# Half of the first x through transposing transfers instead of TensorE, wq right behind them on the SP queue, and a new instruction order

## The chip, the cores and the metric

One core of a Trainium2 chip. The metric is the device time of one execution in microseconds (us): 265.26 us, the median of three runs of the kernel before (265.08 to 267.14). TensorE (PE) multiplies matrices from SBUF into PSUM banks, VectorE (DVE), ScalarE (ACT) and GpSimd (POOL) do the element-wise work, and SyncE (SP) issues transfers. PE, ACT, DVE and POOL each execute their own instructions in order; they meet at semaphores only.

## The reference

Two branches over the same 2048 x 512 input x, mixed per token:

```python
q, k, v = x @ wq, x @ wk, x @ wv          # 32 heads of 16, four segments of 512 tokens
for s in range(4):                        # per segment and head
    a_dot = softmax(q_s k_s^T * 0.25 + causal mask) v_s
    a_mem = (phi(q_s) M) / (phi(q_s) z + 1e-6)      # phi(t) = t + 1 if t > 0 else exp(t)
    o_s = sigmoid(beta) * a_mem + (1 - sigmoid(beta)) * a_dot
    M, z = M + phi(k_s)^T v_s, z + sum(phi(k_s))
a = concat(o) @ wo
b = (gelu(x @ w_gate) * (x @ w_up)) @ w_down        # 512 -> 1792 -> 512
g = sigmoid(sum(x * gate_w))
out = g * a + (1 - g) * b
```

All inputs and the output are bfloat16, the sums in PSUM float32.

## The kernel before

The kernel is built as a list of named tasks. A task is one or several instructions of one engine together with what they read and write. The text `ORDER` at the end of the file gives the order of all tasks, written out by hand: an entry such as `Q0_0:0` is a task and the PSUM bank it opens (there are four banks, `psD0` to `psD3`), and `Qev0_0:a` is a task and the engine that does it (a for ACT, d for DVE). `Emitter` puts each task's instructions on its engine in this order and adds a semaphore wait for each dependency that is not already covered. No planner decides anything when the kernel is built, so the order in the text is the order in which each engine works.

Work is done by segment (s = 0 to 3, 512 tokens each). `project(s)` makes K, Q and V: the tasks `K`, `Q`, `V` with segment and tile are PE matmuls, and `Kev`, `Qev`, `Vev` take them out of PSUM. `kpada` and `kpadb` are DVE copies of K with half the rows masked out. `attend(s, t)` makes scores (`st`, PE, into the four-bank tile psX), their exponentials (`exp`, ACT), the causal mask on the diagonal blocks (`msk`, POOL) and the product with V (`pv`, PE). `vsh` are transfers that put V a second time at the other half of the partitions. `glu_gate(s)` and `glu_up(s)` make the second branch: `G` tasks are PE, seven of them go raw to SBUF (`Gev`) and then through one large ACT instruction (`gelu`, L681), the other seven are read from PSUM by ACT (`gd`, L686). `outputs(s)` multiplies with w_down (`out`) and wo (`wo`), adds, and stores in `dma` tasks. `memory_read`, `memory_write` are the a_mem part (`nd`, `mz`, and the transposing transfers `ktr` and `otr`).

The steps at the start that the change touches:

- The projections need x with its 512 features on the partitions, so x has to be transposed into `xT`. Segments 1 to 3 are loaded by transposing transfers (`ld_xt`, L342 to L346): four for a segment, each of 512 tokens by 128 features, `DMA_TRANSPOSE` on SP.
- Segment 0 is loaded plain into a spare tile and transposed by PE: `ld_x0_0` (128 tokens, SP), `ld_x0_1` (128 tokens, ACT's queue), `ld_x0_2` (256 tokens, SP, behind wk's second half). The tasks `xtr0_01`, `xtr0_00`, `xtr0_10`, `xtr0_11` (L771) are four PE transposes of 128 x 128 each. The first digit is the half of the tokens, the second the half of the features. `xev0_..` (L779 on ACT, L780 on DVE) copy the four results from PSUM to `xT`.
- K of segment 0 is made in pieces (L472): `a` and `b` are the first 256 tokens with features 256 to 511 and 0 to 255, `c` the last 256 tokens. Each piece a or b has two matmuls of 256 columns, each piece c has four; the four tiles make 32 matmuls.
- The weights for Q come in two transfers on SP, `ld_wq0` and `ld_wq1`. SP holds wq0 until wk1 has landed and wq1 until wk0 has landed. wv is held until `x0_2` has landed. These holds are there in `ld_w(..., wait)`:

```python
ld_w("wq0", SP, wq[:, halves[0], :], wsrc(A_wq)[:, halves[0], :], [("wq", 0)], 0.25, ["wk1"])
ld_w("wq1", SP, wq[:, halves[1], :], wsrc(A_wq)[:, halves[1], :], [("wq", 1)], 0.25, ["wk0"])
ld_w("wv", SP, wv[:, :, 0:512], wsrc(A_wv), [("wv",)], 0.5, ["x0_2"])
```

Of the kernel before, what the change touches and what calls it, by code (L numbers as in the profile page):

```python
# [28 lines left out]
R_XT = 3  # L29
# [217 lines left out]
def _build(es, nc, A_x, A_wq, A_wk, A_wv, A_wo, A_beta, B_w_gate, B_w_up, B_w_down, gate_w, out):  # L247
# [69 lines left out]
    def bk(s):  # L317
        return ("bank", s)
# [40 lines left out]
    ld_w("x0_2", SP, pt[stage[0]][:, halves[1], :], xin0[:, halves[1], :], [("xs", 0, 2), ("xs", 0, 3)], 0.25)  # L359
    ld_w("gw", SP, gw4, gate_w.rearrange("(kb p) -> kb p", p=P), [("gw4",), ("gwz",)], 0.01)  # L360
    ld_w("wq0", SP, wq[:, halves[0], :], wsrc(A_wq)[:, halves[0], :], [("wq", 0)], 0.25, ["wk1"])
    ld_w("wq1", SP, wq[:, halves[1], :], wsrc(A_wq)[:, halves[1], :], [("wq", 1)], 0.25, ["wk0"])
    ld_w("wv", SP, wv[:, :, 0:512], wsrc(A_wv), [("wv",)], 0.5, ["x0_2"])
# [100 lines left out]
    def xk(s, i):  # L464
        return [("xT", s % R_XT, i), *([("xT", 0, i, "h0")] if s == 0 else [])]

    def project(s):
        b, b3 = s % 2, s % R_XT
        k0 = [Slot() for _ in range(4)]
        for nm, kbs, h in (("a", (2, 3), 0), ("b", (0, 1), 0), ("c", (0, 1, 2, 3), 1)) if s == 0 else ():  # L470
            for t in range(4):
                one(f"K0_{t}{nm}", PE, len(kbs) * T_MM / 2, [I(lambda e, t=t, i=i, h=h: e.matmul(  # L472
                    BK[k0[t].i][:, 256 * h:256 * h + 256], wk[:, i, t * 128:(t + 1) * 128], xT[0][:, i, 256 * h:256 * h + 256],
                    start=(i == 2 - 2 * h), stop=(i == 1 + 2 * h)), [("xT", 0, i, "h0"), ("wk", i),
                    *([("xT", 0, i)] if h else [])], [bk(k0[t])]) for i in kbs], opens=(nm == "a"))
# [292 lines left out]
    for h in range(2):  # L768
        for p in (1, 0):
            j = 2 * h + p  # L770
            one(f"xtr0_{h}{p}", PE, 4 * T_TR, [I(lambda e, q=q, kb=kb, j=j: e.transpose(  # L771
                XB[:, 1024 * j + (kb % 2) * 256 + (q % 2) * 128:1024 * j + (kb % 2) * 256 + (q % 2) * 128 + 128],
                pt[stage[0]][:, q, kb * 128:(kb + 1) * 128], ident[:, :]),
                [("xs", 0, 2 * h), ("xs", 0, 2 * h + 1), ("pt", stage[0]), ("ident",)], [("X", j)]) for kb in (2 * p, 2 * p + 1) for q in (2 * h, 2 * h + 1)])
            dst = xT[0][:, 2 * p:2 * p + 2, 256 * h:256 * h + 256]
            xin = XB[:, 1024 * j:1024 * j + 512].rearrange("p (k c) -> p k c", c=256)
            wr = [("xT", 0, kb, "h0") if h == 0 else ("xT", 0, kb) for kb in (2 * p, 2 * p + 1)]
            task(f"xev0_{h}{p}", [
                (ACT, 0.477, [I(lambda e, dst=dst, xin=xin: e.activation(dst, xin, ACTF.Copy), [("X", j)], wr)]),  # L779
                (DVE, 0.335, [I(lambda e, dst=dst, xin=xin: e.tensor_copy(dst, xin), [("X", j)], wr)])], L_DVE)  # L780
# [67 lines left out]
ld_x0_0 warm0 warm1:0 ld_x0_1 ident xtr0_01 ld_wk0 masks vones0 causal1 causal0 gwz ld_wk1 ld_x0_2 ld_wq0 xev0_01:d  # L848
ld_gw consts xtr0_00 K0_1a:1 K0_2a:2 K0_3a:3 K0_0a:0 ld_wq1 ld_wv ld_beta xtr0_10 xtr0_11 xev0_00:a K0_2b K0_3b K0_1b
K0_0b xev0_11:a xev0_10:d K0_0c Kev0_0:d kpadb0_0 kpada0_0 K0_3c Kev0_3:a K0_1c K0_2c Kev0_2:d Kev0_1:d kpada0_1  # L850
Q0_0:0 Q0_3:3 Qev0_0:a st0_0A exp0_0A ld_x1_1 ld_x1_0 ld_x1_2 ld_x1_3 gwtr:2 gwev Qev0_3:d phka0_0 Q0_1:1 V0_3b:0
V0_0b:2 V0_2a:3 Vev0_3b:d st0_0B Vev0_0b:d ld_wg0 V0_1a:0 V0_3a:2 phkb0_0 Vev0_2a:d Qev0_1:d Vev0_1a:d Vev0_3a:d
V0_2b:3 Q0_2:1 V0_0a:0 exp0_0B st0_0C exp0_0C V0_1b:2 Vev0_2b:d betab Qev0_2:d Vev0_1b:a bexp Q1_1:3 Q1_2:1 kpadb0_1
Vev0_0a:d causal msk0_0A phkc0_0 vsh0_00 vsh0_01 vsh0_20 Qev1_2:d st0_0D V1_2b:0 G0_1:2 G0_3:1 exp0_0D st0_0E
Vev1_2b:d kpada0_3 exp0_0E V1_3a:0 Vev1_3a:a kpada0_2 Gev0_1:d Gev0_3:d Qev1_1:d G0_5:2 G0_0:1 st0_1A G1_3:3 V1_1b:0
msk0_0B Gev0_5:d vsh0_21 Gev0_0:d Gev1_3:d msk0_0D gqa msk0_0C kpadb0_2 Vev1_1b:d msk0_0E pv0_0:21 exp0_1A st0_1B
gfull tp0_d00 kpadb0_3 V1_0a:3 G0_4:0 msk0_1A G1_0:2 Vev1_0a:d phka0_2 tp0_d01 Gev0_4:d exp0_1B st0_1C exp0_1C msk0_1B
msk0_1C phkb0_2 Q1_0:3 G0_2:1 V1_3b:0 gqb pvp0_00 Qev1_0:d Gev1_0:d Vev1_3b:d Gev0_2:d phkc0_2 ld_wu1 ld_wg1 ld_wu0
ktr0_1 ld_x2_0 st0_1D exp0_1D G1_2:3 K1_0:2 K1_3:0 Gev1_2:d Kev1_3:d st0_2A G0_6:1 V1_2a:3 Vev1_2a:d Gev0_6:d Kev1_0:a
gz0 msk0_1D pv0_1:20 exp0_2A st0_2B exp0_2B ktr0_2 tp0_d10 pvp0_01 tp0_d11 pvp0_10 K1_1:3 Q1_3:1 Qev1_3:d Kev1_1:d  # L860
kpadb1_3 gelu0 G0_7:2 G1_1:0 Gev1_1:d gd0_7 st0_2C G1_4:1 G0_13:3 ktr0_0 Gev1_4:d phka1_0 ld_x2_2 ld_x2_3 G0_9:0
G0_10:1 G0_12:2 gd0_9 gd0_10 gd0_13 gd0_12 G0_8:0 ld_x2_1 vsh1_21 phqa1_0 pvp0_11 vsh1_20 ld_wd1 G0_11:1 K1_2:3
kpadb1_1 ota0_0 Kev1_2:d gd0_8 gd0_11 U0_10:2 V1_0b:0 h0_10 exp0_2C U0_7:1 Q2_1:3 V1_1a:2 ktr0_3 phka1_2 kpada1_3
Vev1_0b:d h0_7 kpada1_2 Qev2_1:d Vev1_1a:a st0_2D exp0_2D U0_11:0 U0_2:1 h0_11 h0_2 phqa1_2 mz0:2 phkb1_0 mza0 phkc1_0
st0_2E U0_4:3 K2_0:0 U0_13:1 h0_4 h0_13 kpada1_0 kpadb1_0 Kev2_0:d exp0_2E st0_3A exp0_3A msk0_2A msk0_2B msk0_2C
msk0_2D msk0_2E U0_9:2 pv0_2:31 st0_3B phkb1_2 exp0_3B h0_9 tp0_d21 G1_5:0 U0_5:2 U0_8:1 Gev1_5:a gr0 phkc1_2 tp0_d20
st0_3C h0_8 K2_3:3 Kev2_3:d U0_3:0 h0_3 pvp0_21 kpada1_1 U0_6:1 h0_5 h0_6 exp0_3C phqb1_2 st0_3D Q2_0:3 Q2_3:0 U0_1:2
exp0_3D Qev2_3:a Qev2_0:d h0_1 pvp0_20 kpadb2_3 st1_0A V2_2b:1 U0_0:3 exp1_0A phqb1_0 h0_0 msk0_3A msk0_3B msk0_3C gz1
goa0 gob0 msk0_3D pv0_3:02 st1_0B exp1_0B tp0_d31 tp0_d30 K2_2:3 U0_12:2 Vev2_2b:d kpadb1_2 Kev2_2:d V2_0b:0 V2_2a:1
st1_0C Vev2_0b:a exp1_0C Vev2_2a:d kpada2_2 h0_12 kpada2_3 phqc1_2 G1_6:3 K2_1:0 Kev2_1:d V2_1b:1 msk1_0B st1_0D  # L870
exp1_0D ld_wd0 kpadb2_1 ktr1_1 vsh1_00 Gev1_6:a out0_1_0:2 out0_0_0:0 st1_0E out0_0_1 out0_1_1 V2_0a:3 exp1_0E
Vev2_1b:d mzq0 Vev2_0a:d out0_0_2 out0_1_2 msk1_0C msk1_0E msk1_0A msk1_0D goc0 G1_8:1 G1_7:3 kpada2_0 ota0_2 wev0_1:d
wev0_0:d gelu1 gd1_7 G1_10:2 ld_x3_2 ktr1_2 ktr1_0 phka2_0 G1_11:0 G1_13:3 vsh1_01 ld_wo ktr1_3 gd1_10 gd1_11 gd1_13
gd1_8 G1_12:2 gd1_12 G1_9:0 ota0_1 pvp0_31 phqc1_0 kpadb2_2 pvp0_30 st1_1A pv1_0:31 tp1_d01 Q2_2:2 Qev2_2:d tp1_d00
ota0_3 gd1_9 V2_3b:0 U1_2:1 U1_9:2 h1_2 Vev2_3b:d pvp1_01 h1_9 pvp1_00 exp1_1A st1_1B phkb2_0 exp1_1B out0_2_0:3
wo0_0:1 V2_1a:0 st1_1C msk1_1B exp1_1C nd1_1:2 out0_2_1 out0_2_2 oev0_0 st1_1D msk1_1C msk1_1A exp1_1D Vev2_1a:a
wev0_2:d ndp1_1 wo0_1:1 out0_3_0:3 V2_3a:2 st1_2A out0_3_1 nd1_3:0 oev0_1 Vev2_3a:a msk1_1D pv1_1:12 exp1_2A st1_2B
dma1 phkc2_0 kpadb2_0 ndp1_3 exp1_2B msk1_2B ld_x3_1 dma0 ld_x3_0 ld_x3_3 tp1_d10 phka2_2 tp1_d11 out0_3_2 pvp1_10
G2_2:0 G2_4:1 wev0_3:a Gev2_4:d Gev2_2:d st1_2C nd1_5:2 G2_0:3 ndp1_5 G2_3:1 G2_1:0 exp1_2C st1_2D exp1_2D msk1_2C
msk1_2A msk1_2D G2_5:2 Gev2_3:d Gev2_1:d Gev2_0:d Gev2_5:d nd1_0:1 G2_6:0 Gev2_6:d nd1_2:3 ndp1_0 ndp1_2 st1_2E  # L880
G2_11:2 wo0_2:0 oev0_2 wo0_3:1 oev0_3 G2_13:3 G2_7:0 G2_10:1 gelu2 gd2_13 gd2_11 G2_8:3 G2_9:2 gd2_10 gd2_7 gd2_8
gd2_9 G2_12:1 K3_0:0 U1_3:3 nd1_4:2 gd2_12 gr1 exp1_2E phqa2_0 pvp1_11 ota1_0 Kev3_0:d ndp1_4 U2_7:1 h1_3 h2_7 U2_11:0
U2_10:2 ota1_1 h2_11 h2_10 st1_3A U2_13:3 U1_4:1 phkb2_2 exp1_3A msk1_2E pv1_2:02 st1_3B phqb2_0 exp1_3B msk1_3B h2_13
h1_4 tp1_d21 tp1_d20 U1_1:3 h1_1 phkc2_2 U1_6:1 U2_9:2 st1_3C U1_8:0 h1_6 U2_3:3 U1_5:1 exp1_3C st1_3D exp1_3D h2_9
h1_8 pvp1_20 h2_3 mz1:2 msk1_3A h1_5 mza1 phqa2_2 msk1_3C U1_0:0 U1_13:3 h1_0 pvp1_21 h1_13 kpada2_1 st2_0A msk1_3D
K3_3:1 U1_7:2 Kev3_3:d pv1_3:03 tp1_d31 h1_7 phqb2_2 dma3 otr1_2 otr1_3 dma2 exp2_0A st2_0B exp2_0B U2_1:1 h2_1 ota1_2
# [26 lines left out]
oev2_2 dma11 dma10 out3_1_1 out3_1_2 msk3_3D otm3_2 otm3_1 wev3_1:a otm3_0 out3_3_0:1 pv3_3:32 out3_0_2 out3_3_1  # L913
wev3_0:a out3_2_0:0 out3_2_1 tp3_d30 tp3_d31 pvp3_31 pvp3_30 ota3_3 otm3_3 wo3_1:3 oev3_1 dma13 wo3_0:2 oev3_0
out3_3_2 out3_2_2 dma12 wo3_3b:3 wev3_3:d oev3_3b wo3_3a:2 wo3_3c:1 oev3_3a dma15b dma15a wev3_2:a oev3_3c dma15c
wo3_2:3 oev3_2 dma14
"""


# [26 lines left out]
```

## Time and profile before

| what | us |
|---|---|
| median of three runs | 265.26 (265.08 to 267.14) |
| the profiled execution, its whole time | 265.46 |
| its span, first to last instruction | 263.7 |
| PE busy in that span | 254.3 |
| DVE busy | 207.9 |
| ACT busy | 197.7 |
| POOL busy | 99.8 |
| DMA queue of SP: 15.68 MB, share of 16 engines | 23.6% |

The lower table is the start of the profiled execution, from the timeline and from the landings of the transfers (us from the start of the span).

| transfer | issue by its queue | landed |
|---|---|---|
| x0_0 (SP) | 0.79 | 3.57 |
| x0_1 (ACT's queue) | 0.78 | 3.74 |
| wk1 (SP) | 1.25 | 5.01 |
| wk0 (ACT's queue) | 1.21 | 5.30 |
| x0_2 (SP) | 1.71 | 5.97 |
| wq0 (SP) | 5.03 | 7.64 |
| wq1 (SP) | 5.89 | 9.88 |
| wv (SP) | 6.33 | 11.34 |
| four transposing transfers of segment 1 (SP) | 7.66, 8.92, 10.21, 11.52 | 11.92, 12.95, 13.64, 14.40 |
| first half of w_gate (SP) | 12.82 | 18.02 |
| four vsh (SP) | 19.70 to 21.75 | 21.89 to 23.82 |
| half of w_up (SP) | 22.40 | 27.57 |

The page gives busy time by engine, the span in 40 slices, the chain of work that ended last, and the costliest groups of instructions. A few PE records are missing in the trace (2775 matmuls are recorded, 2815 weight loads), so a matmul that is missing looks like a short gap of PE. The profiled time outside the span is 265.46 - 263.7 = 1.76 us.

### The profile page before, as it was taken

To read this page: it belongs to the slowest core of one execution; us is meant where nothing else is said; L and a number is where in the kernel's file an instruction comes from. 1 tells how busy PE (TensorE), PEld (TensorE's weight loads), DVE (VectorE), ACT (ScalarE), POOL (GpSimd) and SP (SyncE) were. 2 spreads that over 40 slices of the span, in tenths; PEclk is the share of its full clock that TensorE was granted. 3 is DMA by queue.
4 is the path that set the end of the run, shared out by engine and by line. 5 is a ranking of instruction groups with operands and counts; after the bars stand their busy time and mean duration, and the time that the engine had idled before them with its cause. 6 is when DMAs were issued, how large, how long until landed. Compare 5 with 4: busy or idle time off the path is not lost.

```text
span 263.7 us, 6622 instructions
## 1 busy us (share of the span) xinstructions
PE 254.3 (96%) x2775; PEld 120.4 (46%) x2815; DVE 207.9 (79%) x427; ACT 197.7 (75%) x159; POOL 99.8 (38%) x164
## 2 busy tenths in 40 slices
PE   7999999999999999999999999999999999999994
PEld 4554544444454444444444444444444444444442
DVE  1698979588985866885897999885799967799765
ACT  2487779979888897788967877666889877776611
POOL 5018362054424306440244456436525045264500
PEclk9999999999999999999999999999999999999999
DMA  5855675901015000403103000030143000003302
GB/s 165 221 155 153 197 208 81 290 0 33 1 42 132 0 2 1 102 0 72 31 2 74 9 2 11 22 75 0 22 97 47 0 22 4 2 0 63 80 2 80
DMA packets 31302, 16.50 MB, mean 63 GB/s; under 512 B 20776, under 2 KB 31272, under 8 KB 31272
## 3 DMA queue, kind: packets, MB, share of 16 engines
q1 hardware_dynamic: 30856, 15.68, 23.6%
q8 instruction: 22, 0.36, 0.6%
q10 hardware_dynamic: 416, 0.39, 0.4%
q14 instruction: 8, 0.07, 0.1%
HBM read 8.14 MB, written 2.10 MB: 39 GB/s over the span
## 4 chain that ended last, share of the span: by engine, by line
PE 91%; DVE 3%; DMA 3%; issue 2%; SPq 0%
PE psD L446 45%; PE psD L718 17%; PE psX L598 8%; PE psD L640 7%; PE psD L495 6%; PE psD L732 5%; DMA wq<-in_A_wq_dram 2%; DMA wk<-in_A_wk_dram 1%; PE psD L543 1%; DVE omem L557 1%; DVE ost L736 1%; DVE tT L526 0%; PE psD L573 0%; SPq L340 0%; DVE rcm L556 0%
## 5 line engine op out<-in xcount | busy, mean ns | idle before, releaser
L604 ACT ACTIVATE pt<-psX 128x2048 bf16<-128x2048 f32 x72 | 135.1, 1876 | 41.2 <-PE psX L598 41.0
L610 POOL TENSOR_TENSOR pt<-pt,ctri 128x256 bf16<-128x256 bf16 x128 | 92.2, 726 | 145.3 <-ACT pt L604 117.4
L446 PE MATMUL psD<-xT,wu 128*128 128x512 bf16 x213 | 52.4, 379 | 1.3 <-issue 0.9
L718 PE MATMUL psD<-wd,gb 128*128 128x512 bf16 x213 | 51.8, 379 | 1.2 <-issue 1.0
L446 PE MATMUL psD<-xT,wg 128*128 128x512 bf16 x214 | 51.3, 379 | 1.0 <-issue 0.5
L703 DVE TENSOR_TENSOR gb<-psD,gb 128x512 bf16<-128x512 f32 x56 | 37.4, 680 | 4.9 <-PE psD L446 4.7
L446 PEld LDWEIGHTS psD<-xT,wg 128*128 128x128 bf16 x224 | 20.7, 98 | 24.9 <-issue 1.9
L526 DVE STREAM_TRANSPOSE tT<-psD 128x512 f32<-128x512 f32 x32 | 22.3, 705 | 12.3 <-PE psD L640 12.2
L446 PEld LDWEIGHTS psD<-xT,wu 128*128 128x128 bf16 x224 | 20.6, 98 | 24.1 <-issue 1.7
L718 PEld LDWEIGHTS psD<-wd,gb 128*128 128x128 bf16 x224 | 20.3, 98 | 23.9 <-issue 2.8
L598 PE MATMUL psX<-qT,kD 32*128 32x192 bf16 (+7 forms) x512 | 28.5, 287 | 0.0
L640 PE MATMUL psD<-pt,vnat 64*17 64x128 bf16 (+7 forms) x512 | 18.7, 283 | 0.0
L651 DVE SCALAR_TENSOR_TENSOR ob<-tT,gq,rc 128x256 bf16<-128x256 f32 x32 | 17.8, 556 | 1.1
L495 PE MATMUL psD<-wv,xT 128*128 128x256 bf16 (+1 forms) x128 | 18.5, 273 | 0.0
L640 PE MATMUL psD<-pt,vsh 64*17 64x128 bf16 (+7 forms) x512 | 18.3, 283 | 0.0
L598 PEld LDWEIGHTS psX<-qT,kD 32*128 32x128 bf16 x512 | 8.2, 92 | 21.3 <-ACT pt L604 8.9
L440 DVE CAST gb<-psD 128x512 bf16<-128x512 f32 x24 | 16.0, 681 | 2.4 <-PE psD L446 2.4
L686 ACT ACTIVATE gb<-psD 128x512 bf16<-128x512 f32 x28 | 15.4, 594 | 3.1 <-PE psD L446 2.8
L736 DVE SCALAR_TENSOR_TENSOR ost<-psD,gtok,wds 128x512 bf16<-128x512 f32 (+2 forms) x18 | 12.2, 686 | 6.1 <-PE psD L732 5.3
L440 DVE CAST kT<-psD 128x512 bf16<-128x512 f32 x14 | 9.5, 687 | 8.5 <-PE psD L446 7.3
L446 PE MATMUL psD<-xT,wq 128*128 128x512 bf16 x61 | 15.5, 380 | 0.5 <-DMA wq<-in_A_wq_dram 0.2
L732 PE MATMUL psD<-wo,oT 128*128 128x512 bf16 (+2 forms) x71 | 15.8, 356 | 0.0
(84 smaller groups left out, 258.9 us busy)
## 6 DMA issues: line engine op xcount, KB each, us to landing
out_dram<-ost SPq DMA_DIRECT2D x15, 128.0 KB, 1.8
wg<-in_B_w_gate_dram SPq DMA_DIRECT2D x2, 896.0 KB, 6.3
wu<-in_B_w_up_dram SPq DMA_DIRECT2D x2, 896.0 KB, 5.1
wd<-in_B_w_down_dram SPq DMA_DIRECT2D x2, 896.0 KB, 6.2
vsh<-vnat SPq DMA_DIRECT2D x16, 68.0 KB, 2.1
wq<-in_A_wq_dram SPq DMA_DIRECT2D x2, 256.0 KB, 3.3
wv<-in_A_wv_dram SPq DMA_DIRECT2D x1, 512.0 KB, 5.0
wo<-in_A_wo_dram SPq DMA_DIRECT2D x1, 512.0 KB, 4.5
```

Of the source, the lines that this page charges most:

```text
L440: (DVE, 0.60, [I(lambda e: e.tensor_copy(dst, src()), [bk(sl), *reads], writes)]),
L446: one(name, PE, n * T_MM, [I(lambda e, i=i: e.matmul(BK[sl.i][:, :], lhs(i), rhs(i), start=(i == 0), stop=(i == n - 1)), reads(i), [bk(sl) ...
L495: one(f"V{s}_{m}{'ab'[hf]}", PE, 2 * T_MM, [I(lambda e, i=i, sl=sl, a=a, z=z, xs=xs: e.matmul(BK[sl.i][:, 0:z - a], xs(i), wv[:, i, a:z], ...
L526: one(f"tp{name}", DVE, 0.605, [I(lambda e, sl=sl, ti=ti: e.transpose(tT[ti][:, :], BK[sl.i][:, :]), [bk(sl)], [("tT", ti)])], bias=bias)
L598: ins.append(I(lambda e, t=t, kb=kb, ncol=ncol, c0=c0, g=g: e.matmul(XALL[:, g * 512 + c0:g * 512 + c0 + ncol], kD[b][32 * g:32 * g + 32, ...
L604: one(f"exp{s}_{name}", ACT, 2048 * 0.000833 + 0.05, [I(lambda e: e.activation(pt[slot][:, :, :], xin, ACTF.Exp, scale=ATT_SCALE), [("X",) ...
L610: ins.append(I(lambda e, mv=mv: e.tensor_tensor(mv, mv, cm, ALU.mult), [("pt", slot), ("causal",)], [("pt", slot)]))
L640: ins.append(I(lambda e, kb=kb, slot=slot, c0=c0, n=n, g=g, r0=r0, sl=banks[j], va=va: e.matmul(BK[sl.i][32 * g:32 * g + 17, 64 * kb:512], ...
L651: I(lambda e, ti=ti, ri=ri, t=t, j=j, dst=dst: e.scalar_tensor_tensor(out=dst, in0=t_rows(ti), scalar=gq[:, 2 * t + j:2 * t + j + 1], in1= ...
L703: one(f"h{s}_{ft}", DVE, 0.605, [I(lambda e, sl=sl, gi=gi, f=f: e.tensor_tensor(gb[gi][:, f, :], BK[sl.i][:, :], gb[gi][:, f, :], ALU.mult ...
L718: mm.append(I(lambda e, fb=fb, gi=gi, f=f, q=q, sl=sl: e.matmul(BK[sl.i][:, :], gb[gi][:, f, q], wd[:, fb, :], start=(fb == 0), stop=(fb = ...
L732: one(f"wo{s}_{qt}{sfx}", PE, 4 * T_MM * w / 512, [I(lambda e, kb=kb, q=q, so=so, c=c, w=w: e.matmul(BK[so.i][:, 0:w], oT[:, kb, q], wo[:, ...
```

## The change

Of the four 128-token tiles of segment 0, the first two are still loaded plain and transposed by PE. The last two are loaded by two transposing transfers on SP, `ld_x0_t2` and `ld_x0_t3`, straight into `xT`, each 128 tokens by 512 features. They stand on SP behind wk1, where `ld_x0_2` stood. wq0 and wq1 lose their holds. wv is held until `x0_t3` has landed. The PE transposes fall from 16 to 8, the copies from four to two, both on DVE. K's pieces c now read the two transfers. Last, `ORDER` is another order of all tasks; line numbers behind the loads move by one or two.

```diff
-    ld_w("x0_2", SP, pt[stage[0]][:, halves[1], :], xin0[:, halves[1], :], [("xs", 0, 2), ("xs", 0, 3)], 0.25)
+    for q in (2, 3):
+        load(f"x0_t{q}", SP, lambda e, q=q: e.dma_start_transpose(xT[0][:, :, 128 * q:128 * q + 128], A_x[0, 128 * q:128 * q + 128, :]),
+             [("xT", 0, f"t{q}")], issue=1.31, lat=3.0)
...
-    ld_w("wq0", SP, wq[:, halves[0], :], wsrc(A_wq)[:, halves[0], :], [("wq", 0)], 0.25, ["wk1"])
-    ld_w("wq1", SP, wq[:, halves[1], :], wsrc(A_wq)[:, halves[1], :], [("wq", 1)], 0.25, ["wk0"])
-    ld_w("wv", SP, wv[:, :, 0:512], wsrc(A_wv), [("wv",)], 0.5, ["x0_2"])
+    ld_w("wq0", SP, wq[:, halves[0], :], wsrc(A_wq)[:, halves[0], :], [("wq", 0)], 0.25)
+    ld_w("wq1", SP, wq[:, halves[1], :], wsrc(A_wq)[:, halves[1], :], [("wq", 1)], 0.25)
+    ld_w("wv", SP, wv[:, :, 0:512], wsrc(A_wv), [("wv",)], 0.5, ["x0_t3"])
...
-    for h in range(2):
-        for p in (1, 0):
-            j = 2 * h + p
-            one(f"xtr0_{h}{p}", PE, 4 * T_TR, [I(lambda e, q=q, kb=kb, j=j: e.transpose(
+    for p in (1, 0):
+        one(f"xtr0_{p}", PE, 4 * T_TR, [I(lambda e, q=q, kb=kb, p=p: e.transpose(
...
```

The start of the new order, up to the first scores and a little further (what the loads stand for on SP is the order of the `ld_` entries, without `ld_x0_1` and `ld_wk0`, which are ACT's):

```
ld_x0_1 ld_wk0 vones0 ld_x0_0 ld_wk1 ld_x0_t2 ld_x0_t3 ld_wq0 warm0 ident warm1:0 xtr0_1 xev0_1:d gwz ld_wq1 ld_gw
causal1 masks xtr0_0 xev0_0:d causal0 consts K0_3a:1 K0_1a:2 K0_0a:3 K0_1b K0_2a:0 K0_0b K0_2b K0_3b K0_0c K0_3c K0_1c
Kev0_0:a Kev0_3:a ld_beta ld_wv ld_x1_3 ld_x1_1 ld_x1_0 Q0_0:3 Q0_3:1 Kev0_1:a Qev0_0:a kpada0_0 betab kpadb0_0 st0_0A
Q0_1:2 gwtr:3 bexp exp0_0A kpadb0_3 Qev0_3:d ld_x1_2 gwev K0_2c V0_1a:1 V0_3b:3 Qev0_1:a kpadb0_1 causal Vev0_1a:d
...
```

Around the third segment's gate projection it reads, first before and then after:

```
G2_6:0 Gev2_6:d nd1_2:3 ndp1_0 ndp1_2 st1_2E G2_11:2 wo0_2:0 oev0_2 wo0_3:1 oev0_3 G2_13:3 G2_7:0 G2_10:1 gelu2 gd2_13 gd2_11 G2_8:3
...
G2_3:2 dma1 U1_3:0 ld_x3_3 Vev2_3a:d ld_x3_2 dma0 ld_x3_0 ld_x3_1 Gev2_3:d h1_3 wo0_3:1 st1_2E wev0_3:d oev0_3 msk1_2C msk1_2A msk1_2D msk1_2B G2_10:2 G2_12:0 G2_13:3 gelu2 gd2_10 gd2_12 pvp1_01 kpada2_2 phkc2_2 G2_9:1 G2_11:2
```

## The prediction

> **What bounds the kernel now.** First the page: busy time of the engines and PE's slices.
>
> ```profile
> PE 254.3 (96%) x2775; PEld 120.4 (46%) x2815; DVE 207.9 (79%) x427; ACT 197.7 (75%) x159; POOL 99.8 (38%) x164
> ...
> PE   7999999999999999999999999999999999999994
> ...
> PEclk9999999999999999999999999999999999999999
> ```
>
> PE is full in every slice but the first and the last, at full granted clock in all of them. So nothing is won by making another engine shorter: only less PE work, or fewer gaps of PE at the two ends, can count. Next, the chain of waits in the first 12 us (start, length, what).
>
> ```profile
> 1.25 3.76 DMA wk<-in_A_wk_dram
> 5.01 0.02 issue
> 5.03 0.37 SPq L340
> ...
> 5.89 3.98 DMA wq<-in_A_wq_dram
> 9.88 0.05 issue
> 9.92 1.47 PE psD L446 x6
> ```
>
> The start hangs on two transfers, wk1 landing at 5.01 and wq1 landing at 9.88; after 9.92 the chain is PE alone. Then the timeline of that stretch, for what PE does between.
>
> ```profile
> 5.14 1.03 PE L472 MATMUL psD<-xT,wk 128*128 128x256 bf16 x8 [0.50 <-DMA wk<-in_A_wk_dram]
> ...
> 6.02 0.62 PE L771 MATMUL psX<-ident,pt 128*128 128x128 bf16 x8
> ...
> 6.48 2.78 PE L472 MATMUL psD<-xT,wk 128*128 128x256 bf16 x24
> ...
> 7.66 5.12 SPq L344 DMA_TRANSPOSE xT<-in_A_x_dram  x4
> ...
> 9.31 0.38 PE L446 MATMUL psD<-xT,wq 128*128 128x512 bf16 x1
> 9.92 1.47 PE L446 MATMUL psD<-xT,wq 128*128 128x512 bf16 x6 [0.23 <-DMA wq<-in_A_wq_dram]
> ```
>
> From these: eight transposes take 6.48 - 6.02 = 0.46 us of PE. A 256-column matmul follows the last after 0.109 us ((2.78 - 0.27) / 23), a 512-column one after 0.216. One of the eight Q matmuls is missing in the records (7 are shown): K ends at 6.48 + 24 x 0.109 = 9.10, so Q starts there, the second is the one at 9.31, the third was due at 9.53 and started at 9.92. That is the only wait of PE after 5.14: 0.39 us. Later gaps in the PE timeline are 0.05 or 0.16 us, each put down to issue or a missing record.
>
> Last, ACT's rows of the large gelu and the landings of segment 1's transposing transfers.
>
> ```profile
> L681 ACT ACTIVATE gb<-gb 128x3584 bf16<-128x3584 bf16 x4 | 12.8, 3191 | 0.0
> L681 ACT ACT_TABLE_LOAD x4 | 5.1, 1283 | 0.1
> ```
>
> ```profile
> DMA to landing us min/median/max: 2.9/3.7/4.3
> ```
>
> **What the change removes.** Eight PE transposes: -0.46 us, all on the path, since PE is the path. The two copies behind them (0.42 DVE, 0.60 ACT) lay beside PE: nothing. The number of PE instructions is otherwise the same (2815 to 2807), and in both orders PE passes 164 times between matmuls on the whole array and on parts of it, so the pieces that PE does, and what it costs to pass between them, are equal. The holds of wq0 and wq1: up to -0.39 us, if wq1 then lands before it is due.
>
> **The start, step by step.** Up to wk1's landing nothing is moved on SP, so K starts at 5.14 again. The two copies to xT are now both on DVE, the second after the first and a 0.11 us memset: 4.45 + 0.42 + 0.11 + 0.42 = 5.4. It is due, with wk0 (landed 5.30), at the seventh matmul, 5.14 + 6 x 0.109 = 5.79 (wk0 was due at 6.48 before). Sixteen matmuls end the first half at 5.14 + 1.74 = 6.88; then t2 and t3 are due. SP issues t2 at 1.71 (where x0_2 was) and, at 1.26 + 0.04 us an issue (5.12 / 4), t3 at 3.01. No row has this form; the nearest four are segment 1's, 2.9 to 4.3 from issue to landing, the longer ones behind wv in the queue. So t3 lands between 5.9 and 7.3. I take 6.4, since only wk1 is ahead: no wait, bounds 0 and 0.4.
>
> wq0 is issued at 4.31, wq1 at 4.73 (before 5.03, 5.89). From issue to landing they took 2.61 and 3.99 (behind each other). So wq1 lands by 8.7, and is due two matmuls into Q, 5.14 + 28 x 0.109 + 0.43 = 8.62 (four K matmuls, `K0_2c`, are moved behind). I take no wait, because back-to-back transfers leave out wq1's separate start; the other end is below, as a rival. Q's first bank needs `Kev0_0` on ACT: 20 matmuls end at 7.32, + 0.2 + 0.60 = 8.12, due 8.19. `betab` now stands on DVE ahead of `kpadb0_0`, and behind it the first scores wait: beta, issued about 5.65 instead of 6.84, lands behind wq1, by 8.9; + 4 copies (0.5) + 0.35 = 9.75, scores due at 8.19 + 8 x 0.216 + 0.1 = 10.02. Covered, by 0.3.
>
> Behind the new hold of wv on SP stand the four transposes of segment 1 and w_gate. wv at 6.4 + 5.0 (its row) = 11.4, due 10.02 + 0.32 (scores) + 0.86 (Q) + 0.48 (the rest of K, gate weights) = 11.7; before due 12.55. Segment 1's last is issued at about 6.9 + 3 x 1.3 = 10.8, lands by 15.1, due 15.5 (17.8 before). These margins are thinner than before, but the transfers come no later.
>
> **The new order behind the start.** PE had no wait there, so the order can only add. I went through ACT's, DVE's and SP's orders with the rows' durations, and one place comes out short: the third segment's gelu. From the end of `G2_3`: 0.2 to DVE, 0.68 `Gev2_3`, 0.04, 1.28 table load, 3.19 gelu, 0.60 `gd2_10`, less 0.17 for ACT's overlaps, 0.06 back to PE: 5.88 us until `G2_11` has its bank. In the new program the table load stands behind the wait for DVE. PE has `U1_3`, `wo0_3`, four gate tiles (6 x 0.863) and `st1_2E` (0.31): 5.49. So PE waits 0.39, bounds 0 (if ACT loads its table early) and 0.4; I take 0.35. Before, PE had as much work there and no wait. For places that come out within 0.1 I add 0.1.
>
> The end: before, the last 128x512 `oev` starts 0.2 after PE and its transfer lands 1.69 after issue at 261.39. Now the two small pieces (0.66 us of PE) come after it; on DVE 0.26 + 0.40 more, on SP two issues more, and 1.5 to land: from the end of the 512 piece 3.23 instead of 2.67, and this end is 0.66 earlier. 0.1 less; I take 0.
>
> **Sum.** -0.46 - 0.39 + 0.35 + 0.1 = -0.40 on the profiled 265.46, so 265.06. That execution stands 0.20 above the median of the runs, so the forecast is 264.9.
>
> **Rivals.** (1) Nothing new waits: without the 0.45, and with 0.1 from the end, 264.3 to 264.5. For it: PE never waited in 250 us before, and the table load of this gelu stood ahead of the wait before (116.65, right behind an exponential). Against it: the 5.88 against 5.49.
>
> (2) The transfers at the start are late. t3 at 7.3 costs 0.4; if wq0 lands 0.8 behind that and wq1 2.24 behind wq0 (the distance before), wq1 lands at 10.3, 1.7 late, so 265.3 to 266.6. For it: wq1's 3.99; against it: wk's two halves landed 0.29 apart.
>
> (3) Many small waits in the new order, at several places of 0.1 to 0.3: 265.2 to 266.2. For it: PE has no idle time that could take them in. Against it: rows put them within 0.1.
>
> (4) Slower: the vsh transfers. The half of w_up that is held until w_gate's first half has landed now stands ahead of them on SP, before it stood behind. w_gate is issued at about 12.1 and lands 5.2 later (its row), 17.3; w_up 5.2 after that, 22.5; the vsh behind it by 24.0; due at the first `pv`, 25.6 (26.55 before). It decides when they land after 25.6. If both loads take 7.5, as the longest such row (23.05 to 30.55), they land at 27.1 and more: a wait of 1.5 to 2.2, and 266.4 to 267.1. Against it: that longest row was behind another 896 KB.
>
> (5) Slower by much: blocks are transposed one after another. If each of the eight 128 x 128 blocks took the 1.26 us of one issue, t3 would land at 1.71 + 10.1 = 11.8, 4.9 after 6.88: 269.8. Against it: segment 1's sixteen blocks landed between 11.92 and 14.40, at most 0.2 us a block. The Trainium skill, page "VectorE: DVE Perf Modes", sections "The three transpose paths" and "Rules for kernel authors", speaks against the change in this way: it gives 390 ns for a 128 x 128 transpose on TensorE and 1309 ns by DMA, and advises TensorE where PSUM can take the result. By its figure eight in a row would be 10.5 us, an estimate of 270.2; the trace does not bear it out, neither for the DMA nor for TensorE, where eight took 0.46 us.
>
> **Chances.** Forecast (264.6 to 265.2) 0.50, (1) 0.12, (2) 0.15, (3) 0.12, (4) 0.09, (5) 0.02. The range 264.2 to 266.5 holds the forecast, (1), (3) and nearly all of (2). 1% is 2.65 us, about what tells a change from none here: faster by that (under 262.6) would need more than three times the 0.85 that is removed, 0.02. Slower (over 267.9) is (5) and (4) where both loads are later than any row: 0.05. The rest, 0.93, is within 1%.
>
> **What would show it.** Right: K starts at 5.1, no PE idle between 5.2 and the first scores at about 10.0, wq1 landed before 8.6, t3 before 6.9; one PE gap of some 0.3 us before a gate matmul near 119 us that ACT's `gd` ends, with a table load starting only after `Gev2_3`; PE busy about 253.9. Wrong: PE idle on `x0` or wq in the first 10 us, a first `pv` waiting for vsh, or PE gaps ended by DVE or ACT that sum to more than 0.5 us.

## The result and the profile after

| | us |
|---|---|
| before, median of 20 runs | 265.36 (265.05 to 267.14) |
| after, median of 20 runs beside them | 266.50 (265.68 to 267.45) |
| ratio | 1.0034, 95% interval 1.0022 to 1.0046 |
| profiled execution of after | 266.26, span 264.5 (before 265.46, span 263.7) |

The change costs 1.14 us by the medians, 0.80 between the two profiled executions. The forecast was 264.9, a gain. The ratio, here and below, is an estimate from all the runs and not the quotient of the two medians, which is 1.0043 here.

From the page of after, the rows that were shown of before:

```profile
PE 259.0 (98%) x2807; PEld 119.9 (45%) x2807; DVE 203.8 (77%) x422; ACT 199.2 (75%) x162; POOL 97.4 (37%) x164
...
PE   8899999999999999999999999999999999999995
...
PEclk9999999999999999999999999999999999999999
```

PE looks busier by 4.7 us, but no matmul record is missing here (2807 of 2807), where 40 were missing in before; the two sums can't be set against each other. The rows on the start say more. The chain of waits of after (start, length, what):

```profile
5.49 0.42 SPq L340
5.90 0.04 issue
5.95 3.87 DMA omem<-in_A_beta_dram
9.82 0.02 issue
9.85 0.16 DVE betab L748
...
10.62 0.36 DVE kD L485
10.98 0.05 issue
11.03 0.40 PE psX L599 x4
```

The chain no longer goes through wq. It goes through SP's issues, the 3.87 us that beta's transfer took, DVE's four copies of it and one mask multiply behind them (`kpadb0_0`), to the first scores at 11.03. The timeline of PE and DVE there (start, length, what, idle time before it and what ended it):

```profile
4.90 3.46 PE L474 MATMUL psD<-xT,wk 128*128 128x256 bf16 x28
8.27 1.90 PE L448 MATMUL psD<-xT,wq 128*128 128x512 bf16 x8
11.03 0.40 PE L599 MATMUL psX<-qT,kD 32*128 32x512 bf16 x4 [0.86 <-DVE kD L485]
```
```profile
8.16 0.35 DVE L485 TENSOR_SCALAR kD<-kT,maskA 128x512 bf16<-128x512 bf16 x1 [2.91 <-ACT kT L441]
9.85 0.74 DVE L748 COPY betab<-omem 32x8 bf16<-32x8 bf16 x4 [1.34 <-DMA omem<-in_A_beta_dram]
10.62 0.61 DVE L485 TENSOR_SCALAR kD<-kT,maskB 128x512 bf16<-128x512 bf16 x2
```

The eight transposes and the wait for wq1 are gone: Q runs back to back from 8.27. In their place PE stands idle for 0.86 us before the first scores (0.93 against the usual distance). DVE could have made that mask at 8.5; it stood behind `betab` for 1.34 us instead.

Later there is one PE gap of more than 0.1 us. PE's timeline has it, and ACT's timeline shows its cause:

```profile
122.17 2.12 PE L448 MATMUL psD<-xT,wg 128*128 128x512 bf16 x9 [0.22 <-ACT gb L687]
```

```profile
117.14 1.28 ACT L682 ACT_TABLE_LOAD   x1 [0.83 <-DVE gb L442]
118.44 3.19 ACT L682 ACTIVATE gb<-gb 128x3584 bf16<-128x3584 bf16 x1
```

The table load of the third segment's gelu waits for DVE's last copy, though it needs nothing from it. `G2_11` started 0.38 us late, at 122.17 (against the usual distance between two matmuls). In before the same load stood right behind an exponential, without a wait:

```profile
116.65 1.28 ACT L681 ACT_TABLE_LOAD   x1
117.94 3.19 ACT L681 ACTIVATE gb<-gb 128x3584 bf16<-128x3584 bf16 x1
```

### The profile page after: what moved, and what is told of

The parts are those of the page before. It is cut to its first block, busy times and chain, and to the rows that moved or that the text cites. A ratio compares the mean times of both kernels' runs of the same rounds, so it can differ in the third digit from the quotient of the medians.

```text
span 264.5 us, 6634 instructions
## 1 busy us (share of the span) xinstructions
PE 259.0 (98%) x2807; PEld 119.9 (45%) x2807; DVE 203.8 (77%) x422; ACT 199.2 (75%) x162; POOL 97.4 (37%) x164
## 3 DMA queue, kind: packets, MB, share of 16 engines
q1 hardware_dynamic: 31672, 15.68, 24.8%
## 4 chain that ended last, share of the span: by engine, by line
PE 92%; ACT 2%; SPq 2%; DMA 1%; DVE 1%; issue 0%; DVEq 0%; ACTq 0%
PE psD L448 45%; PE psD L719 19%; PE psX L599 9%; PE psD L641 7%; PE psD L496 6%; PE psD L733 5%; DMA omem<-in_A_beta_dram 1%; PE psD L544 1%; ACT gb L682 1%; SPq L360 1%; SPq L340 1%; PE psD L574 1%; ACT L682 0%; DVE ost L737 0%; DVE gb L442 0%
## 5 line engine op out<-in xcount | busy, mean ns | idle before, releaser
L611 POOL TENSOR_TENSOR pt<-pt,ctri 128x256 bf16<-128x256 bf16 x128 | 89.9, 710 | 146.7 <-ACT pt L605 140.7
L448 PE MATMUL psD<-xT,wu 128*128 128x512 bf16 x224 | 54.6, 380 | 0.0
L719 PE MATMUL psD<-wd,gb 128*128 128x512 bf16 x224 | 53.7, 380 | 0.0
L448 PE MATMUL psD<-xT,wg 128*128 128x512 bf16 x224 | 52.7, 380 | 0.2 <-ACT gb L687 0.2
L442 DVE CAST gb<-psD 128x512 bf16<-128x512 f32 x23 | 15.4, 679 | 3.4 <-PE psD L448 3.3
L448 PE MATMUL psD<-xT,wq 128*128 128x512 bf16 x64 | 16.3, 380 | 0.0
L496 PEld LDWEIGHTS psD<-wv,xT 128*128 128x128 bf16 x128 | 11.7, 97 | 7.3 <-issue 1.5
```

Of the source, the lines that this page charges most:

```text
L448: one(name, PE, n * T_MM, [I(lambda e, i=i: e.matmul(BK[sl.i][:, :], lhs(i), rhs(i), start=(i == 0), stop=(i == n - 1)), reads(i), [bk(sl) ...
L496: one(f"V{s}_{m}{'ab'[hf]}", PE, 2 * T_MM, [I(lambda e, i=i, sl=sl, a=a, z=z, xs=xs: e.matmul(BK[sl.i][:, 0:z - a], xs(i), wv[:, i, a:z], ...
L611: ins.append(I(lambda e, mv=mv: e.tensor_tensor(mv, mv, cm, ALU.mult), [("pt", slot), ("causal",)], [("pt", slot)]))
L719: mm.append(I(lambda e, fb=fb, gi=gi, f=f, q=q, sl=sl: e.matmul(BK[sl.i][:, :], gb[gi][:, f, q], wd[:, fb, :], start=(fb == 0), stop=(fb = ...
```

## The experiments

Twelve kernels ran, each beside runs of the kernel before on the same chip, and each with a profile. Three quantities of each profile are gathered here first, since they answer most questions at once: when PE's first 256-column matmul (or 128-column transpose) is spaced by the short distance, 0.109 (0.056) us in place of 0.213 (0.107) ("fast from" in the table; the text calls it the moment at which the fast pace, or the pace, comes); the start of the first scores; and the time from there to the end of the span. The kernels are explained one by one behind the table.

| profile of | its time | K starts | fast from | first scores | from there to the end |
|---|---|---|---|---|---|
| before | 265.46 | 5.14 | 4.31 | 11.33 | 252.42 |
| before, holds off | 265.36 | 5.14 | 5.86 | 11.19 | 252.41 |
| before, filled | 265.74 | 5.16 | 6.60 | 11.60 | 252.43 |
| new loads, old order | 267.13 | 5.42 | 10.01 | 12.92 | 252.45 |
| the same, filled | 264.85 | 5.38 | 5.38 or earlier | 10.69 | 252.43 |
| the same, two warm-ups | 265.71 | 5.04 | 7.54 | 11.54 | 252.43 |
| after | 266.26 | 4.90 | 5.47 | 11.03 | 253.52 |
| after, filled | 266.46 | 5.73 | 6.94 | 11.23 | 253.51 |
| betab late | 267.56 | 5.22 | 6.23 | 10.63 | 255.22 |
| betab at the idle place | 266.03 | 4.99 | 6.65 | 10.72 | 253.58 |
| table first | 267.34 | 5.36 | 10.00 | 12.48 | 253.10 |
| table first and betab late | 266.93 | 5.18 | 5.75 | 10.37 | 254.84 |
| table first and betab at the idle place | 265.09 | 4.95 | 5.70 | 10.21 | 253.15 |
| the same, filled | 265.39 | 5.17 | 4.30 | 10.20 | 253.46 |

The last column hardly depends on what the start did: 252.41 to 252.45 in the order of before, whatever else differs. In the new order it is 253.5 as changed and 253.1 without the gelu's gap; the two kernels with betab late and the last row have further waits of their own there, told below. What a run adds lies in front of the first scores, and what the order adds lies behind them.

**Betab late.** In the order, for the changed kernel:

```
- ... Qev0_0:a kpada0_0 betab kpadb0_0 st0_0A Q0_1:2 gwtr:3 bexp exp0_0A ...
+ ... Qev0_0:a kpada0_0 kpadb0_0 st0_0A Q0_1:2 gwtr:3 exp0_0A ...
- exp0_0C st0_0D ...
+ betab exp0_0C bexp st0_0D ...
```

> The changed kernel with two entries of its order moved: betab (DVE's four copies of beta, which wait for beta's transfer) from ahead of kpadb0_0 to ahead of exp0_0C, and bexp from ahead of exp0_0A to behind exp0_0C. Theory: beta's landing at 9.82 and the copies behind it hold kpadb0_0 and so the first scores, 0.93 us beyond the usual distance between matmuls. Then the first scores start at 10.2 to 10.3 instead of 11.03, and the time falls by 0.9, from 266.3 to about 265.4, level with the kernel before. Rival: what is late next is wv (landed 11.29) or segment 1's transposes, and takes most of it back: a fall of at most 0.4, to 265.9 or more, with a new PE gap before the first V.

267.35, ratio 1.0067 (1.0043 to 1.0090): slower still. The first scores did come earlier, at 10.63, though the pace came 0.76 later than in after. But the place was badly chosen. PE's and DVE's timelines of this kernel:

```profile
20.85 1.46 PE L448 MATMUL psD<-xT,wg 128*128 128x512 bf16 x6 [0.99 <-DVE betab L748]
```
```profile
20.25 0.73 DVE L748 COPY betab<-omem 32x8 bf16<-32x8 bf16 x4
21.59 0.20 DVE L764 RECIPROCAL gq<-gq 128x8 f32<-128x8 f32 x1 [0.61 <-POOL gq L763]
```

DVE had no idle time there, and the chain that hangs on `betab` (ACT's `bexp`, POOL, then a reciprocal on DVE) was now due at once: DVE waited 0.61 for it, PE 0.99 and once more 0.42. Neither theory foresaw this, and the run doesn't tell what beta costs.

**Table first.** Where an ACT instruction waits for two counters, ACT's own goes to the end of the list of waits:

```
-            for k, (sem, v) in req.items():
+            for k, (sem, v) in sorted(req.items(), key=lambda r: eng == ACT and r[1][0] is self.cnt[ACT]):
```

> The changed kernel with one thing else: where an ACT instruction waits for ACT's own counter and for DVE's, the wait for its own comes first, so that the table load of a gelu, which is placed behind the first wait, no longer stands behind the wait for DVE. Theory: the third segment's gelu starts 1.28 us earlier after its last copy, and PE's gap of 0.38 us near 122 us closes: the time falls by 0.3 to 0.4, to about 265.9. Rival: the gap is not the table load's, or is taken back by what comes behind it (the gelu's consumers are then late at the next place): no fall, within 0.1 of the changed kernel.

266.24, ratio 1.0024 (0.9999 to 1.0049). By time alone it can't be told from after; the trace tells it. ACT's timeline:

```profile
117.79 1.28 ACT L682 ACT_TABLE_LOAD   x1
119.08 3.19 ACT L682 ACTIVATE gb<-gb 128x3584 bf16<-128x3584 bf16 x1
```

In the trace this turns the two waits round: in after the wait for DVE stands ahead of the table load and the one for ACT's own counter at the gelu itself; here the one for ACT's own stands ahead of the load and the one for DVE at the gelu. So it is the end of the list that is waited for first. The load now follows the exponential without a wait, no PE gap over 0.05 us is left behind the first scores, and the last column falls by 0.42. The same profile showed something that the prediction had left out. PE's timeline:

```profile
5.36 5.46 PE L474 MATMUL psD<-xT,wk 128*128 128x256 bf16 x28 [0.56 <-DVE xT L779]
10.66 1.89 PE L448 MATMUL psD<-xT,wq 128*128 128x512 bf16 x8
```

The same 28 matmuls that took 3.46 us in after take 5.46 here, without a gap: 0.213 apart until 10.0, then 0.109. Four of its 12 runs lie at 267.3 to 267.5, the other eight at 265.8 to 266.3.

**Both** (the two edits together).

> The edits of the two kernels before this one together. Theory: the two waits add, 0.9 + 0.35, so about 265.0, which is 0.3 under the kernel before. Rival (many small waits in the new order, each too small to be seen): the sum of the two is found, but the time stays at or above the kernel before, 265.4 or more.

266.91, ratio 1.0038 (1.0018 to 1.0058). Missed, for the reason that betab late missed: PE waits 1.57 us at 21.32.

**New loads, old order.** The changed kernel's program with the order of before; the names of the dropped or split tasks alone are adapted:

```
- ... ld_wk1 ld_x0_2 ld_wq0 xev0_01:d
+ ... ld_wk1 ld_x0_t2 ld_x0_t3 ld_wq0 xev0_1:d
- ... ld_beta xtr0_10 xtr0_11 xev0_00:a K0_2b K0_3b K0_1b
+ ... ld_beta xev0_0:a K0_2b K0_3b K0_1b
- K0_0b xev0_11:a xev0_10:d K0_0c ...
+ K0_0b K0_0c ...
```

> The change without its new order: the transposing transfers of the third and fourth tile, the two transposes on PE that are left, and the holds of wq0 and wq1 off, but everything in the order of the kernel before. Theory: the loads by themselves save the transposes and the wait for wq1, 0.46 + 0.39 = 0.85, and the order adds what the change lost: about 264.5, and at most 264.9 if PE's first matmuls run at the slow distance for longer, as they did in the changed kernel (+0.24). Rival: the transposing transfers make the other transfers of the start late in any order (wq1 or wv then ends a PE wait): 265.2 or more, no faster than the kernel before.

265.31, ratio 0.9993 (0.9968 to 1.0018): by the median, the rival. But the runs spread from 264.58 to 267.13, and nothing in the trace waits for a transfer behind K's start; K's 32 matmuls take 5.84 us, fast only from 10.0. So the next three kernels ask whether the pace makes the spread.

**Filled.** Five more warm-up matmuls where PE stood idle between its first transposes and K. Here on the kernel before; on the old-order kernel the same lines:

```
+    s1 = Slot()
+    one("warm2", PE, 0.4, [I(lambda e: e.matmul(BK[s1.i][:, 0:P], warm[:, :], warm[:, :], start=True, stop=True),
+                             [("warm",)], [bk(s1)]) for _ in range(5)], bias=9000.0, opens=True)
...
- ld_gw consts xtr0_00 K0_1a:1 ...
+ ld_gw consts xtr0_00 warm2:0 K0_1a:1 ...
```

> The kernel before with five more warm-up matmuls (128 x 128 by 128 columns, on the zeros of the first six) between the first eight transposes and the first K matmul, where PE stood idle. Theory: PE runs at half pace until about 3.4 us of enough activity are behind it (the change to the fast pace came at 4.3 to 6.2 us in four traces, at 9.95 to 10.0 in the two whose times are 267.1 and 267.3); with the idle stretch filled no run has the late change. So none of the 12 runs is above 266.6, where 7 of 35 of the kernel before were at 267.2 or more; the median moves little, 265.1 to 265.4. Rival: the runs above 267 are not the pace's: again about a fifth of them. The Trainium skill, page "TensorE: Matmul & The Clock Gate", Part 1, states such a gate with a free-running window of 3413 ns; the traces' changes between 4.3 and 10.0 agree with it.

> The old-order kernel (the changed loads in the order of before) with the same five warm-up matmuls. Theory: its runs at 266.8 to 267.1 (3 of 12) go, the rest spread over 264.5 to 265.6 as the fast pace comes at 4 to 7 us, since no wait for wq1 absorbs it now; median 264.9, that is 0.4 to 0.5 under the kernel before. Rival: the change's loads are worth nothing, and it stays at 265.3.

Before, filled: 265.77 (264.98 to 265.98), ratio 0.9988 (0.9967 to 1.0008). Old order, filled: 264.84 (264.47 to 265.46), ratio 0.9970 (0.9957 to 0.9984). The runs above 266.6 are gone from both (none of 24; 4 of 35 of before beside them), as the theory said. For one kernel alone that could be chance (the 7 of 35 of the expectation are 5 of 35 in the runs); but in all four filled kernels together none of 43 runs is above 266.65, while 13 of the 125 unfilled runs of before are above 267. The median of before filled was expected at 265.1 to 265.4 and is higher. The second is the fastest kernel of this study, below both that it was made from. PE's timelines, the kernel before filled, then the old order filled:

```profile
4.63 0.74 PE L383 MATMUL psD<-warm 128*128 128x128 bf16 x5
5.16 1.71 PE L475 MATMUL psD<-xT,wk 128*128 128x256 bf16 x8
6.71 0.61 PE L774 MATMUL psX<-ident,pt 128*128 128x128 bf16 x8
7.15 2.78 PE L475 MATMUL psD<-xT,wk 128*128 128x256 bf16 x24
9.77 1.89 PE L449 MATMUL psD<-xT,wq 128*128 128x512 bf16 x8
```
```profile
4.47 0.74 PE L385 MATMUL psD<-warm 128*128 128x128 bf16 x5
5.38 3.65 PE L477 MATMUL psD<-xT,wk 128*128 128x256 bf16 x32 [0.16 <-DMA wk<-in_A_wk_dram]
8.87 1.89 PE L451 MATMUL psD<-xT,wq 128*128 128x512 bf16 x8
```

In the first, six K matmuls and part of a seventh run at the long distance, and Q starts at 9.77. That is late enough for wq1, which landed at 10.04 and was not waited for. So the wait for wq1 in the kernel before is also a cover: a late pace goes into it at no cost.

**Two warm-ups.** `for _ in range(6)` becomes `for _ in range(2)` in the old-order kernel's `warm1`.

> The old-order kernel (the changed loads in the order of before) with two warm-up matmuls in place of six, so that PE stands idle between about 1.9 and 3.7 us. Theory: PE's fast pace then needs its 3.4 us of activity after that, and comes at 8 to 11 us in every run: all K and most of Q run at half pace, and the time is 265.8 to 267.5 in all runs, median 266.6, against 265.3 with six and 264.8 with eleven. Rival: the pace does not hang on the warm-up matmuls: 265.3, with a quarter of the runs near 267, as with six.

266.44 (265.71 to 267.90), ratio 1.0047 (1.0016 to 1.0078). The median is the theory's; the profile is of the fastest of the seven runs, and in it the pace comes at 7.54, earlier than the 8 to 11 of the theory. The same work with eleven, six and two warm-up matmuls, on three chips: medians 264.84, 265.31, 266.44, ratios to before 0.9970, 0.9993, 1.0047. A single profile need not follow that order (10.01 with six, 7.54 with two). In the runs as a whole the pace hangs on the activity ahead of it, and the time on the pace.

**Betab at the idle place, alone, with the table first, and filled.** In the order of the changed kernel:

```
- ... kpada0_0 betab kpadb0_0 st0_0A Q0_1:2 gwtr:3 bexp exp0_0A kpadb0_3 Qev0_3:d ld_x1_2 ...
+ ... kpada0_0 kpadb0_0 st0_0A Q0_1:2 gwtr:3 exp0_0A kpadb0_3 Qev0_3:d betab ld_x1_2 ...
- ... st0_0B exp0_0B V0_0a:1 ...
+ ... st0_0B exp0_0B bexp V0_0a:1 ...
```

> The changed kernel with the ACT wait order of the table-first run, and betab put where DVE was idle in the traces (behind Qev0_3, at about 11 us), bexp behind exp0_0B, where ACT was idle. Theory: both waits of the changed kernel are gone and none comes in their place, so its profiled account falls by 0.93 + 0.38 to about 264.95 where PE gets its fast pace as early as in the changed kernel's profile (5.45 us); where the pace comes later, nothing absorbs it, so runs spread from 264.6 up to about 266, with a few above 266.8, median 265.3 to 265.6. Rival: many small waits of the new order keep it at 266 or more with the gaps closed.

> The changed kernel with both mended places (table first, betab at DVE's idle place) and the five warm-up matmuls. Theory: 264.6 to 265.6, median 265.0, no run above 266.3. Rival: small waits of the new order, 265.6 or more in the median.

> The changed kernel with only betab and bexp moved to the idle places of DVE and ACT (as in the betab-idle run, but with ACT's waits as the change has them). Theory: the wait for beta alone is worth 0.9 to 1.3 (in six traces of this queue order beta landed at 9.5 to 10.3, and first scores come 1.2 behind it), and the gelu's 0.37 stays: median 265.4 to 265.7, first scores at 10.2. Rival: beta's wait only covers others, 266.0 or more.

Alone: 265.56, ratio 1.0009 (0.9992 to 1.0026). With the table first: 265.14, ratio 0.9997 (0.9977 to 1.0017), and 2 of 12 runs above 266.8. Filled: 265.26 (264.93 to 265.88), ratio 0.9986 (0.9969 to 1.0003). All three medians are where the theory put them, or up to 0.3 beside it. In the profile of betab alone the first scores come at 10.72 and not at the expected 10.2: the pace came at 6.65 and Q ended late. With the table first, PE's timeline is:

```profile
8.39 1.89 PE L448 MATMUL psD<-xT,wq 128*128 128x512 bf16 x8
10.21 0.39 PE L599 MATMUL psX<-qT,kD 32*128 32x512 bf16 x4
```

No PE gap over 0.05 us is left after K's start, and the new order, so mended, is level with before by the ratio (its median is 0.41 lower). beta landed at 10.28 in this execution, behind the start of the first scores. The filling takes nothing more off the median here. The filled one shows a wait that the others don't:

```profile
16.58 0.61 PE L451 MATMUL psD<-xT,wq 128*128 128x512 bf16 x2 [0.20 <-DMA xT<-in_A_x_dram]
```

Segment 1's last transposing transfer landed at 16.53 in that execution, at 14.2 to 14.9 in the other traces of the new order.

**The changed kernel filled,** with the same lines behind `xtr0_0`.

> The changed kernel with five more warm-up matmuls and nothing else. Theory: its first scores hang on beta's landing (+ 1.2 us) and not on PE's pace, so the median stays, 266.1 to 266.6, and only runs above 267.2 go. Rival: it is the late fast pace that makes the changed kernel slow: the median falls to 265.8 or lower.

266.38 (265.91 to 266.65), ratio 1.0032 (1.0021 to 1.0044). The number is the theory's, its reason only in part: in this profile wk1 landed at 5.60 and the pace came at 6.94, so Q ended late and beta, landed at 9.56, was not waited for. The pace and beta's transfer run side by side, and the later of them sets the first scores.

**Before, holds off.** `["wk1"]` and `["wk0"]` are dropped from the loads of wq0 and wq1.

> The kernel before with only the holds of wq0 and wq1 taken away (their transfers are issued without waiting for wk1 and wk0). Theory: the one wait of PE in the start, 0.39 us for wq1, goes, but it also hid up to 0.39 us of a late fast pace, so the median falls by 0.1 to 0.4, to 265.0 to 265.3, and the lowest runs by the whole 0.39, to about 264.6. The runs above 267 stay. Rival: without the holds wk or x's second half land later and take it back, 265.5 or more.

265.63 (265.05 to 265.87), ratio 0.9992 (0.9971 to 1.0012). Missed: wq1 landed at 7.45 and PE doesn't wait for it, yet the median doesn't fall, and the lowest run is 265.05, not 264.6. No run is above 267 (2 of 23 of before beside it), which so few runs can't tell from chance. The interval leaves room for 0.8 us of gain and 0.3 of loss.

## Why the prediction was wrong

**The step that failed** is beta's: "beta, issued about 5.65 instead of 6.84, lands behind wq1, by 8.9; + 4 copies (0.5) + 0.35 = 9.75, scores due at ... 10.02. Covered, by 0.3." It was issued at 5.95 and landed at 9.82, 1.17 behind wq1; in eight traces of this queue order it landed between 9.35 and 10.28. The copies took 0.74. The first scores were due at 10.02 and came at 11.03: K's start 0.25 earlier, + 0.24 for the pace, + 0.07 for `Kev0_0`, + 0.93 for beta.

The price of beta is shown by the move of `betab` alone: 1.0034 to 1.0009, 0.25% or 0.66 us by the ratios (0.94 by the medians, of runs that were not taken side by side); the two intervals just overlap, so the size is rough. The traces show the wait itself gone: with `betab` moved, in betab late, both and table first with betab at the idle place, the first scores came at 10.63, 10.37 and 10.21 where beta landed at 10.20, 10.14 and 10.28; the 1.20 us that lie between the two in after would have put them at 11.3 to 11.5.

The 8.9 was argued from wq1's landing. The only row for this transfer itself (6.84 to 11.69 in before, 4.85 us) would have given 5.65 + 4.85 = 10.5, and it was not used, not even as an end of the range; no rival had it either. The prediction named PE gaps ended by DVE or ACT of more than 0.5 us together as a sign of being wrong, and that is what came (0.93 and 0.38), but it had put the first of the two at nothing.

**The pace** was taken from one execution. "A 256-column matmul follows the last after 0.109" holds for a run in which PE was fast at 4.31, and the row of 9s that the prediction read as full clock does not show when that is (last section). In the 14 profiles it comes between 4.3 and 7.5, and twice at 10.0; each us behind K's start costs half a us where no wait covers it. That made 0.24 of the profiled 0.80. It also undercut the second term, "up to -0.39" for wq1: the wait that was removed had been hiding late paces, and the holds alone gave nothing that could be measured. Together with the transposes, filled against filled, the loads gave 265.77 - 264.84 = 0.93 by the medians, side by side on one chip (0.48 by the ratios); 0.85 was forecast. So their size was about right where the pace comes early, but not term by term. Between the two profiles, 11.60 and 10.69, the transposes are 0.45, the first K matmuls of before filled, at the long distance, 0.67, and K's later start in the other takes 0.22 back; neither waits for wq1.

**Right, with their sizes.** The transposing transfers landed at 5.69 and 6.14 (6.4 was taken), wq1 at 8.65 (8.7): no wait. The gelu's gap was put at 0.35 "with a table load starting only after `Gev2_3`"; it is 0.38, and the table-first kernel closes it. The vsh landed at 23.3 to 24.8, before 25.6: rival (4) fell, and (5), blocks one after another, by 0.45 us between two transfers of four blocks.

**Too small** was the "+ 0.1" for the new order. From the first scores on, it takes 253.10 to 253.15 without the gelu's gap, before 252.42; 0.44 of the 0.7 are the four matmuls of `K0_2c`, which it has moved there, so the rest is 0.24 to 0.29. That is 0.14 to 0.19 more than forecast, less than rival (3), and that it is many small waits is not shown. About 0.1 of it lies at the end, which the prediction took as 0: from the start of the last group of wo matmuls to the end of the span it is 5.19 in after and 5.17 in table first with betab at the idle place, against 5.09 in before filled, whose records are complete.

**The account.** Between the profiled executions: -0.46 transposes, -0.39 wq1, -0.25 K's start, +0.24 pace, +0.07 `Kev0_0`, +0.93 beta, +0.38 gelu, +0.28 the rest of the order: +0.80, as measured (`K0_2c` falls out, 0.44 less in front of the first scores and 0.44 more behind). K's start is the luck of this execution: with the new loads it lies between 4.90 and 5.73 in eleven profiles, with the old ones at 5.14 to 5.16 in three; and the pace is one draw of many. Set against the medians, if the usual run ends as the profiled ones do: 266.50 is first scores at 11.26 (less 253.52 and the 1.72 outside the span), 265.36 is first scores at 11.23 (less 252.42 and 1.71). In the usual run the change then brings the first scores no earlier at all, though 0.85 was to be saved in front of them and 0.44 of K was moved behind them; beta and the pace take all of it. The 1.10 behind them (that K, 0.38 gelu, 0.28) is what is left as the loss. Of that the gelu's share is shown by an edit; of the 0.28, some 0.1 is the end, and the rest stays unexplained.

## What to carry to other kernels

A wait that is removed was perhaps hiding something: ask what else ended just before it, and in which of several runs. Moving a small copy ahead on an in-order engine moves its input's deadline too, so find that input's issue-to-landing time in the trace and use it as it stands, however small the transfer. In a kernel whose start is at half pace, keep the engine occupied from its first instruction to the first real one; five matmuls on zeros took 0.5 us off the median of the new loads in the old order. In the other three kernels that were filled they took away the late runs but moved the median by -0.1 to +0.2 only: in before and after another wait (for wq1, for beta) covers the pace, and for the third the reason is not shown.

## What the runs showed of the hardware that was not expected

PE's matmuls run at half pace at first: 0.213 us for 256 columns until some moment, 0.109 from then on. The moment moved from run to run, 4.3 to 6.65 us with six warm-up matmuls (10.0 in two of nine profiles), 7.5 with two, at most 6.94 with eleven. The granted-clock row doesn't show it: all its digits are 9 in the page of the table-first kernel, in whose second slice (6.6 to 13.3 us) all matmuls up to 10.0 are at the long distance. The Trainium skill, page "TensorE: Matmul & The Clock Gate", Part 1, states a gate that halves PE's clock until one window of 3413 ns has been busy, and that the window runs freely, so that the moment varies. The distances (0.107 and 0.056 for 128 columns) are the page's own, the two profiles at 10.0 lie 3.35 us behind the latest of the others with six warm-ups, about one such window, and filling the idle stretch took the late runs away, which agrees; the window itself no run here shows. The page calls the ramp less than 1% of a typical span; here it is up to 2.2 us (12.92 against 10.69 for the first scores of the old-order kernel without and with the fill), 0.8%, twice what the whole change did.

A transfer of few bytes is not a quick one: beta, 64 bytes to each partition, took 3.4 to 4.3 us from issue to landing in eight traces with the new order, 4.85 in before.
